# One first-layer product in another PSUM bank, and three sets of copies given to ScalarE, in a fused attention and feed-forward kernel

## The chip, the cores and the metric

The kernel runs on one NeuronCore of a Trainium2 chip. The engines named below are TensorE (PE, with its weight loads listed apart as PEld), VectorE (DVE), ScalarE (ACT), GpSimd (POOL) and SyncE (SP). Each works through its own list of instructions in order, and waits where an instruction needs a semaphore that another engine or a transfer raises. The metric is the time of one execution on the device in microseconds; the kernel before took 298.02 us, the median of 5 runs between 297.35 and 299.05.

## The reference

Attention over a sliding window (each token sees the 32 on either side of it), 8 batches of 576 tokens, 8 heads of 64, and behind it a two-layer feed-forward product with a sigmoid form of GELU, on all 4608 tokens:

```python
scores = scale * np.matmul(q, k.transpose(0, 1, 3, 2))
mask = np.abs(pos[:, None] - pos[None, :]) <= window          # window = 32
scores = np.where(mask, scores, -1000000000.0)
attn = np.exp(scores - np.max(scores, axis=-1, keepdims=True))
attn = attn / (np.sum(attn, axis=-1, keepdims=True) + 1e-09)
attn_out = np.matmul(attn, v)
...
x = attn_out.transpose(0, 2, 1, 3).reshape(4608, 512)
h = x @ w_in                                                  # 512 x 2048
g = h * (1.0 / (1.0 + np.exp(-1.702 * h)))
return g @ w_out                                              # 2048 x 512
```

## The kernel before

The tokens are taken as 36 units of 128 queries, and two units make one tile of 256 tokens for the feed-forward part. A unit passes through these steps: `scores` (PE multiplies keys with queries, ACT takes the exponential), `band` (DVE multiplies the mask in), `values` (PE multiplies with the values), `norm` (DVE divides by the sum: a reciprocal and a product for each half of the heads, which give the tile `x`), and `x_T` (x is transposed on PE, and an engine copies it from PSUM into the tile `xT`; from unit 8 on a transposing DMA does this). Then `layer1(t, d)` makes an eighth of the first layer of tile t: 8 matmuls into one PSUM bank (`h_ps`, line 332), and one ACT instruction that applies the GELU and writes `g` (line 334). `layer2`, and from tile 3 on `product`, make the second layer.

**PSUM.** The eight banks are dealt out by `bank` under four names: two called h (for first-layer products), one o, one t, and four called a, which scores and values use in turn. Under one name the banks go round: a new use waits until the use before it in the same bank has been read out. With two h banks, the third `layer1` in a row waits for the GELU of the first.

**The values.** A unit's 128 queries are two blocks of 64, and the second block needs keys that start 64 tokens later. So each 128 rows of values stand in SBUF twice: as loaded (`ve`, a ring of eight), and shifted by 64 rows (`vo`). `odd_v(m, eng)` makes the shifted copy by two copies of 64 partitions x 528 elements: the lower half of `ve[m]`, and the upper half of `ve[m + 1]`. It must come after the loads of both and before `values(m)`.

**The order** is written out by hand: the engines run their instructions in the order in which the program issues them. `head` handles units 0 to 6 and prepares the operands; then `window(4)` to `window(19)` follow. Three places matter here.

- In `head`, lines 511 to 525: first-layer products of tile 0 stand between the values of units 2 and 3 and their transposes: `layer1(0, 0)`, `values(2)`, `norm(2)`, `layer1(0, 1)`, `values(3)`, `norm(3)`, `x_T(2)`, `layer1(0, 2)`, `x_T(3)`, `layer1(0, 3)`, then tile 1. This is where ACT changes from the exponential to the GELU, and so loads another function table.
- In `head`, lines 552 to 578: `x_T(4)` and `x_T(5)` stand between the last pieces of the second layer of tiles 0 and 1, and `layer1(2, 0)` after them needs both copies. In the kernel before, unit 4's copy is DVE's and unit 5's is ACT's.
- In `window(4)`: after the scores of units 7, 8 and 9, the call `gelu_table` makes ACT load the GELU table ahead of need, by an activation of one element (`spark`). DVE masks and divides for units 7 to 9. `x_T(7)` is transposed on PE and copied by ACT, two `layer1` of tile 3 follow, DVE pairs the heads of the fourth block of queries and keys (eight copies, `qc` and `kc`), and makes the shifted values of units 10 and 11 (line 643). Then four rounds follow of `keys_T`, `queries_T` and a `layer1`. All four `keys_T` are transposed into the one t bank, so a round's transposes wait until DVE has copied the keys of the round before into `kT`.

Of the kernel before, what the change touches and what calls it, by code (L numbers as in the profile page):

```python
# [15 lines left out]
F32 = mybir.dt.float32  # L16
# [12 lines left out]
class _Kernel:  # L29
# [290 lines left out]
        self.cast(eng or nc.vector, out, tp)  # L320


    def layer1(self, t, d):
        nc = self.nc
        if d == 0:
            self.g[t] = self.work.tile([128, self.NFF, 256], F16, name="g", tag="g", bufs=2)
        hps = self.bank("h", [128, 2, 256], F32, "h_ps")
        ffs = (d, d + 8) if t > 2 else (2 * d, 2 * d + 1)
        for i in range(2):
            ff = ffs[i]  # L330
            for kr in range(self.NK):
                nc.tensor.matmul(hps[:, i, :], self.w_in_sb[:, kr, ff * 128:(ff + 1) * 128], self.xT[t][:, kr, :],  # L332
                                 start=(i == 0 and kr == 0), stop=(i == 1 and kr == self.NK - 1))
        nc.scalar.activation(self.g[t][:, ffs[0]:ffs[1] + 1:ffs[1] - ffs[0], :], hps, AF.Gelu_apprx_sigmoid)  # L334
# [105 lines left out]
    def head(self):  # L440

        nc, dve, act, pool = self.nc, self.nc.vector, self.nc.scalar, self.nc.gpsimd
# [72 lines left out]
        self.values(3)  # L515
        self.norm(3)
        self.x_T(2, "t")
        self.layer1(0, 2)
        self.x_T(3, "o")
        self.layer1(0, 3)  # L520
        for d in range(4):
# [13 lines left out]
        def run(n):  # L535
            for _ in range(n):
                l2.pop(0)()
# [20 lines left out]
        self.norm(5)  # L558
        self.band(6)
        run(1)  # L560
        self.x_T(4, "a")
        run(1)
        self.x_T(5, "a", act)
        run(1)
# [30 lines left out]
    def window(self, w):  # L595
        nc, dve, sp = self.nc, self.nc.vector, self.nc.sync
        a, b = 2 * w, 2 * w + 1
        att = w < self.NW
        t, act = w - 2, nc.scalar
        l1 = [(lambda d=d: self.layer1(w - 1, d)) for d in range(8)] if w <= self.NW else []  # L600

        def run(lst, n=1):
            for _ in range(min(n, len(lst))):
                lst.pop(0)()

        def loads():
            for m in (2 * w + 6, 2 * w + 7):
                if m < self.NU:
                    self.load_v(m)
            if w % 2 == 0 and 512 * (w // 2 + 3) < self.N:  # L610
                self.load_keys(w // 2 + 3)
                self.load_heads(w // 2 + 3, "q")

        if w == 4:
            l2 = [(lambda u=u, i=i: self.layer2(u, i, "oh"[u % 2], (dve, act)[u % 2])) for u in (4, 5) for i in range(4)]
            self.scores(7)
            self.scores(a)
            run(l2, 3)
            self.band(7)
            self.scores(b)  # L620
            run(l2)
            self.band(a)
            self.values(7, "th")
            self.gelu_table()
            self.band(b)
            self.norm(7)
            run(l2, 2)
            self.values(a)
            self.values(b)
            run(l2)  # L630
            self.x_T(7, "t", nc.scalar)
            self.norm(a)
            self.x_T(a)
            self.norm(b)
            self.x_T(b)
            run(l2)
            loads()
            run(l1, 2)
            for c in "qk":
                for hp in range(4):  # L640
                    self.pair_heads(c, 3, hp, dve)
            for m in (10, 11):
                self.odd_v(m, dve)
            run(l1, 2)
            for hp in range(4):
                self.keys_T(3, hp)
                self.queries_T(3, hp, "a", nc.scalar)
                run(l1)
            self.g_sums(w - 1, 0)
            self.feed(w)  # L650
            return
        loads()
        if not att:
            self.close(w, l1)
            return
        self.scores(a)
        if w > 5:
            self.scores(b)
        self.g_sums(t, 1, (0, 1))
        self.product(t, 1, "o")  # L660
        self.keep(t, 1, dve)
        self.product(t, 2, "h")
        if w == 5:
            self.scores(b)
        self.g_sums(t, 1, (2, 3))
        self.result(t, 11)
        self.gelu_table()
        self.product(t, 5, "t")
        self.band(a)
        self.product(t, 6)  # L670
        self.band(b, 0)
        self.keep(t, 6, dve)
        self.band(b, 1)
        run(l1)
        self.values(a)
        self.values(b)
        self.norm(a)
        self.x_T(a)
        self.product(t, 7)
        self.keep(t, 7, dve)  # L680
        self.result(t, 22)
        run(l1, 1)
        self.product(t, 4)
        self.result(t, 21, act)
        self.norm(b)
        self.x_T(b)
        self.product(t, 3)
        self.result(t, 12)
        run(l1, len(l1) - 4)
        self.g_sums(w - 1, 0)  # L690
        self.feed(w)
        run(l1, 4)
# [109 lines left out]
```

## Time and profile before

| What | Value |
|---|---|
| median of 5 runs | 298.02 us (297.35 to 299.05) |
| the profiled execution: its time, and its span from first to last instruction | 297.74 us, 295.5 us |
| PE matmul busy | 287.5 us, 97% of the span |
| DVE busy | 196.8 us, 67% |
| ACT busy | 186.9 us, 63% |
| POOL busy | 86.6 us, 29% |
| granted TensorE clock | full in the whole span |
| a first-layer product's GELU on ACT (128x512) | 595 ns, 144 of them |
| a copy to `vo` on DVE (64x528) | 303 ns on average |
| an instruction that loads an activation table | 1283 ns |

A profile page tells how long each engine was busy, and follows the chain of work that ended last back to the start. "PE busy" is a share of pipelined matmuls, whose ends are modelled: a matmul row can look busy while the next is held back. So waits of PE are better read from the starts of matmuls and weight loads than from the busy share. A row of the timeline has the start and the length in us, the engine, the line, the operation, output and input with their shapes, and the number of instructions merged into the row; in brackets stands how long the engine was idle before it and what ended that.

### The profile page before, as it was taken

The page shows a single profiled execution, that of the slowest core. Times are in us where ns is not written, and L with a number is a line of the kernel's source. Part 1 is how long each engine was busy: PE and PEld are TensorE (multiplying, and loading weights), DVE is VectorE, ACT ScalarE, POOL GpSimd, SP SyncE. Part 2 cuts the span into 40 slices and gives each one's busy share as a digit, 9 for nine tenths or more (in the row PEclk, how much of TensorE's full clock was granted, in tenths as well). Part 3 has the DMA queues.
Part 4 walks back from the last instruction along what each step waited for, and adds up shares of the span by engine and source line. Part 5 has one row for each costly group of instructions (what it writes and reads, how often), then busy time and mean ns, then how long its engine had stood idle before and what let it go on. Part 6 is the DMA issues. An engine that isn't in the chain of part 4 may idle for free.

```text
span 295.5 us, 9582 instructions
## 1 busy us (share of the span) xinstructions
PE 287.5 (97%) x4052; PEld 236.3 (80%) x4052; DVE 196.8 (67%) x589; ACT 186.9 (63%) x309; POOL 86.6 (29%) x127
## 2 busy tenths in 40 slices
PE   8889999999999999999999999999999999999994
PEld 3568755775788888888888888888888888888884
DVE  3563457788796867586768676858685858583352
ACT  4676537686684848485858585757575757575330
POOL 8876425968438011911161011202000000000000
PEclk9999999999999999999999999999999999999999
DMA  9999999999999997999499939691953030303012
GB/s 148 147 206 206 199 184 133 193 176 185 155 168 116 162 164 145 135 170 203 69 156 180 204 38 142 109 158 26 143 109 106 3 108 10 104 9 100 2 71 71
DMA packets 118649, 37.76 MB, mean 128 GB/s; under 512 B 96080, under 2 KB 114256, under 8 KB 118608
## 3 DMA queue, kind: packets, MB, share of 16 engines
q0 software_dynamic: 75888, 18.16, 76.1%
q1 hardware_dynamic: 42272, 18.62, 31.1%
q8 instruction: 31, 0.51, 0.7%
q10 hardware_dynamic: 448, 0.39, 0.5%
q14 instruction: 10, 0.08, 0.1%
HBM read 36.96 MB, written 9.44 MB: 157 GB/s over the span
## 4 chain that ended last, share of the span: by engine, by line
PE 88%; DVE 5%; ACT 2%; DMA 2%; POOL 1%; issue 1%; POOLq 0%; DVEq 0%
PE h_ps L332 41%; PE o_ps L394 31%; PE o_ps L344 6%; PE sc L263 4%; PE pv L292 3%; PE tp L176 2%; DMA ve<-in_v_dram 2%; DVE x L304 1%; ACT p L269 1%; DVE vo L106 1%; DVE qc L106 1%; DVE kT L106 1%; PE tp L319 0%; DVE p L281 0%; ACT L334 0%
## 5 line engine op out<-in xcount | busy, mean ns | idle before, releaser
L332 PE MATMUL h_ps<-xT,w_in_sb 128*128 128x256 bf16 x1152 | 135.8, 273 | 0.7 <-ACT g L334 0.7
L334 ACT ACTIVATE g<-h_ps 128x512 f16<-128x512 f32 x144 | 85.6, 595 | 74.0 <-PE h_ps L332 72.7
L332 PEld LDWEIGHTS <-w_in_sb 128*128 128x128 bf16 x1152 | 111.9, 98 | 14.3 <-issue 0.9
L157 POOL DMA_DIRECT2D ve<-in_v_dram x40 | 34.0, 861 | 100.3 <-PE pv L292 89.1
L394 PEld LDWEIGHTS <-gs 128*128 128x128 f16 x480 | 45.9, 98 | 5.7
L394 PE MATMUL o_ps<-w_sum,gs 128*128 128x256 f16 x360 | 44.4, 273 | 0.0
L269 ACT ACTIVATE p<-sc 128x512 bf16<-128x512 f32 x72 | 37.2, 604 | 2.7 <-PE sc L263 2.5
L394 PEld LDWEIGHTS <-g 128*128 128x128 f16 x360 | 34.2, 98 | 4.5 <-ACT g L334 0.2
L371 DVE TENSOR_TENSOR gs<-g 128x512 f16<-128x512 f16 x30 | 12.7, 422 | 31.6 <-ACT g L334 31.6
L304 DVE TENSOR_TENSOR x<-pv,rec 128x256 bf16<-128x256 f32 x72 | 30.6, 425 | 2.5
L394 PE MATMUL o_ps<-w_out_sb,g 128*128 128x256 f16 x240 | 29.1, 273 | 0.0
L412 DVE TENSOR_TENSOR o_sb<-o_ps,part 128x256 f32<-128x256 f32 x45 | 19.0, 422 | 12.0 <-PE o_ps L394 11.4
L106 DVE COPY part<-o_ps 128x256 f32<-128x256 f32 x45 | 19.1, 424 | 11.8 <-PE o_ps L394 10.4
L281 DVE TENSOR_TENSOR p<-p,mask 128x512 bf16<-128x512 bf16 x64 | 24.8, 427 | 1.2 <-ACT p L269 1.0
L344 PE MATMUL o_ps<-w_out_sb,g 128*128 128x512 f16 x96 | 23.2, 380 | 0.0
L106 DVE COPY vo<-ve 64x528 bf16<-64x528 bf16 x65 | 19.7, 303 | 2.8 <-DMA ve<-in_v_dram 1.3
L146 POOL DMA_DIRECT2D ks<-in_k_dram x22 | 18.6, 871 | 3.6 <-DMA qs<-in_q_dram 2.0
L431 ACT ACT_TABLE_LOAD x15 | 19.2, 1283 | 0.3
L269 ACT ACT_TABLE_LOAD x15 | 19.2, 1283 | 0.3
L303 DVE RECIPROCAL rec<-pv 128x4 f32<-128x4 f32 x72 | 12.6, 175 | 9.9 <-PE pv L292 9.9
L106 DVE COPY kT<-tp 128x512 bf16<-128x512 bf16 (+3 forms) x24 | 12.2, 530 | 7.0 <-PE tp L176 6.4
L292 PEld LDWEIGHTS <-p 128*64 128x64 bf16 x576 | 11.1, 110 | 6.4 <-DVE p L281 3.2
(69 smaller groups left out, 260.6 us busy)
## 6 DMA issues: line engine op xcount, KB each, us to landing
out_dram<-o_sb SPq DMA_DIRECT2D x34, 256.0 KB, 2.8
ve<-in_v_dram POOLq DMA_DIRECT2D x32, 128.0 KB, 5.8
ks<-in_k_dram POOLq DMA_DIRECT2D x19, 128.0 KB, 8.6
w_in_sb<-in_moe_w_in_dram POOLq DMA_DIRECT2D x4, 512.0 KB, 10.8
w_out_sb<-in_moe_w_out_dram POOLq DMA_DIRECT2D x4, 512.0 KB, 12.0
qs<-in_q_dram POOLq DMA_DIRECT2D x2, 448.0 KB, 11.5
qs<-in_q_dram POOLq DMA_DIRECT2D x3, 256.0 KB, 8.5
qs<-in_q_dram POOLq DMA_DIRECT2D x2, 384.0 KB, 11.0
```

Of the source, the lines that this page charges most:

```text
L106: (eng.copy if eng is self.nc.scalar else eng.tensor_copy)(out, in_)
L157: self.nc.gpsimd.dma_start(self.ve[m % NV][off:off + n, :, :self.D], self.v[b, :, s:s + n, :].rearrange("h s d -> s h d"))
L269: nc.scalar.activation(p[:, eo].rearrange("k h (s j) -> k h s j", j=JT), sc[eo].rearrange("k h (j s) -> k h s j", j=JT), AF.Exp, scale=sel ...
L281: self.nc.vector.tensor_mul(pv, pv, msk.to_broadcast([128, 4, 2, SQ]))
L292: nc.tensor.matmul(acc[half][blk * 64:blk * 64 + 64, hh, :], p[:, h % 2, h // 2 * 2 + blk, :], vt[:, h, :D + 1], start=(hh == 0), stop=(hh ...
L304: nc.vector.tensor_mul(x[:, hs, :], acc[half][:, :, :D], rec[:, hs, :].to_broadcast([128, 4, D]))
L332: nc.tensor.matmul(hps[:, i, :], self.w_in_sb[:, kr, ff * 128:(ff + 1) * 128], self.xT[t][:, kr, :], start=(i == 0 and kr == 0), stop=(i = ...
L334: nc.scalar.activation(self.g[t][:, ffs[0]:ffs[1] + 1:ffs[1] - ffs[0], :], hps, AF.Gelu_apprx_sigmoid)
L344: nc.tensor.matmul(o_ps, self.g[t][:, ff, s * 128:(s + 1) * 128], self.w_out_sb[:, ff, :], start=(ff == 0), stop=(ff == self.NFF - 1))
L394: nc.tensor.matmul(self.part[t, key], x, y, start=(first and k == 0), stop=(k == 7), skip_group_check=True)
L412: self.nc.vector.tensor_add(dst, self.part[t, src], self.part[t, other])
L431: self.nc.scalar.activation(self.spark, self.spark, AF.Gelu_apprx_sigmoid)
```

## The change

Three edits in the order of work; nothing is computed otherwise.

- `layer1` takes the name of the bank as an argument. `layer1(0, 2)` uses one of the four banks called a instead of an h bank.
- The copy of unit 4's transposed x goes from DVE to ACT.
- The four copies that make the shifted values of units 10 and 11 go from DVE, where they stood behind the pairing of the heads, to ACT, where they stand right after the early load of the GELU table and ahead of the copy of unit 7's transposed x.

```diff
-    def layer1(self, t, d):
+    def layer1(self, t, d, kind="h"):
         nc = self.nc
...
-        hps = self.bank("h", [128, 2, 256], F32, "h_ps")
+        hps = self.bank(kind, [128, 2, 256], F32, "h_ps")
...
         self.x_T(2, "t")
-        self.layer1(0, 2)
+        self.layer1(0, 2, "a")
         self.x_T(3, "o")
         self.layer1(0, 3)
...
-        self.x_T(4, "a")
+        self.x_T(4, "a", act)
         run(1)
         self.x_T(5, "a", act)
...
             self.gelu_table()
+            for m in (10, 11):
+                self.odd_v(m, act)
             self.band(b)
             self.norm(7)
...
                     self.pair_heads(c, 3, hp, dve)
-            for m in (10, 11):
-                self.odd_v(m, dve)
             run(l1, 2)
```

PE, POOL and SP keep their instructions in the same order. DVE has five copies fewer and ACT five more.

## The prediction

> **What bounds the kernel.** I read three views in turn: the chain of waits on the page, PE's waits, and the timeline around each wait that the change touches. The chain:
>
> ```profile
> PE 88%; DVE 5%; ACT 2%; DMA 2%; POOL 1%; issue 1%; POOLq 0%; DVEq 0%
> ```
>
> PE's issue order is the bound; 12% of the chain is something else. Where? The busy times by stretch give PE 211.00 of 211.00 us between 79 and 290 us, so nothing can be won or hidden there: whatever time PE reaches 79 us early, it ends early, if no load is late. Before 20 us the change does nothing. Between 20 and 80 us the idle times of the weight loads are:
>
> ```profile
> engine line waited for: us in total, times, longest us
> ...
> PEld L176 <- DVE kT L106: 0.9, 1, 0.9
> PEld L332 <- issue: 0.9, 1, 0.9
> ...
> PEld L332 <- DVE xT L106: 0.4, 1, 0.4
> ```
>
> These are one stall in a set of key transposes, and two in first-layer products. Each edit touches one of them.
>
> **Edit A, the bank of `layer1(0, 2)`.** The timeline at 21 us:
>
> ```profile
> 21.49 0.40 PE L319 MATMUL tp<-ident,x 128*128 128x128 bf16 x4
> ...
> 21.67 0.10 PEld L332 LDWEIGHTS <-w_in_sb 128*128 128x128 bf16 x1
> ...
> 21.98 1.09 ACT L334 ACTIVATE g<-h_ps 128x512 f16<-128x512 f32 x2
> ...
> 22.63 1.03 PE L332 MATMUL h_ps<-xT,w_in_sb 128*128 128x256 bf16 x8 [0.75 <-ACT g L334]
> ```
>
> The weights of `layer1(0, 2)` are loaded at 21.67, and its first matmul starts only at 22.63, after the first GELU (21.98 + 0.60 = 22.58), which had waited for four exponentials and a table load. Four transposes start 0.055 us apart (21.49 to 21.67), so the matmul could have started at 21.72: the wait costs 22.63 - 21.72 = 0.91 us. In the a bank nothing holds it: the bank's use before was the first half of `values(2)`, which DVE read at 20.33 to 20.75.
>
> What is late next? Eight matmuls (0.109 each, from 1.03 = 7 steps + 0.27) issue until 22.59. Then `x_T(3)` needs both halves of x(3), which DVE finishes at 22.11 and 22.66; its last two transposes wait some 0.06. `layer1(0, 3)` then starts near 22.82, against 23.73 before. It takes the h bank whose GELU ended at 22.58; `layer1(1, 0)` at 23.69 takes the one read by 23.07 and needs DVE's copy of x(3), due about 23.45. So **A gains 0.91 us**. Further on, the weights and heads that PE meets before 53 us land ahead of it: the last quarter of `w_in` at 12.4 + 12.6 = 25.0, used about 30; the paired queries of block 1, DVE's at 36.51 to 37.67, first used at 38.0 when shifted. One load becomes late, that of the values 7 (issued 34.50, 10.5 to landing: 45.0). DVE's sixth odd copy would reach it at 44.3; the mask behind it then shifts by 0.4 instead of 0.91, but ends by 47.2, and the values product that needs its first two instructions starts about then with those done since 46.2. No cost.
>
> **Edit B, x of unit 4.**
>
> ```profile
> 53.30 0.11 PEld L332 LDWEIGHTS <-w_in_sb 128*128 128x128 bf16 x2 [0.39 <-DVE xT L106]
> ```
>
> The row says 0.39, but PE was still issuing: its last second-layer matmul started at 53.02, and such steps are 0.216 us, so the product could have started at 53.24. The wait is 0.06 us. On ACT, unit 4's copy (0.59) fits into the 0.53 of idle time ahead of unit 5's (52.58 to 53.17), which then ends in time for 53.24; if ACT's two copies don't overlap at all, unit 5's ends some 0.05 later and the gain is gone. **B: -0.06**, bounds -0.06 and +0.05. The DVE time freed reaches nobody who waits.
>
> **Edit C, the odd values.** What it removes from DVE, and what it adds to ACT:
>
> ```profile
> 69.26 0.20 ACT L431 ACTIVATE spark<-spark 128x1 f32<-128x1 f32 x1
> ...
> 71.74 0.59 ACT L106 COPY xT<-tp 128x512 bf16<-128x512 bf16 x1 [2.28 <-PE tp L319]
> ...
> 72.40 3.66 PE L332 MATMUL h_ps<-xT,w_in_sb 128*128 128x256 bf16 x32
> ...
> 75.59 1.67 DVE L106 COPY vo<-ve 64x528 bf16<-64x528 bf16 x4
> ...
> 77.19 0.81 DVE L106 COPY kT<-tp 128x512 bf16<-128x512 bf16 x2
> ...
> 78.05 0.23 PEld L176 LDWEIGHTS <-kc 128*128 128x128 bf16 x4 [0.95 <-DVE kT L106]
> ```
>
> *Removed.* The second round's transposes wait for the t bank, which DVE empties at 77.19 to 78.00, behind the four copies. PE itself was free when the first round's product had been issued: it starts at 76.34, and eight steps of 0.109 end at 77.21. The stall is 78.05 - 77.21 = 0.84 us. Without the copies DVE starts on `kT` as in the next rounds, 0.43 us after the first transpose (78.05 to 78.48), so at 75.90 + 0.43 = 76.33, ends at 77.14, and PE follows at about 77.20: nothing of the stall is left. Later rounds keep pace with PE (1.3 us each).
>
> *Added.* The four copies go into ACT's idle 2.28 us (69.46 to 71.74), and what is queued behind them is the copy of unit 7's x, for which all of tile 3's first layer waits: it ends at 72.33 and PE starts at 72.40 without a pause. So the cover has no slack. Does it hold? Copies of this kind on ACT exist in the head of the trace:
>
> ```profile
> 11.04 1.28 ACT L106 COPY vo<-ve 64x528 bf16<-64x528 bf16 x2
> ```
>
> Two of 0.63 take 1.28, so they start 0.65 apart. By this row four take 3 x 0.65 + 0.63 = 2.58 and end at about 72.06, and x(7) follows. A copy from PSUM behind one from SBUF began 0.09 before the latter's end (qT at 6.50, behind a cast that ran from 5.98 to 6.60), so x(7) runs from 71.97 to 72.56 instead of 72.33: PE loses 0.2. The Trainium skill speaks for less: "ScalarE: Activation LUTs", section "What ACT_TABLE_LOAD costs", has back-to-back instructions overlap by about 93 ns. Then they are 0.535 apart, start at about 69.37, end at 71.60, and cost nothing. The trace has such overlap where ACT reads PSUM (two GELUs in 1.09 us, at 21.98), but not in the one pair that reads SBUF. I take the row: +0.2, bounds 0 and +0.4.
>
> A rule of the same page speaks against C: "Rules for kernel authors" wants simple arithmetic on VectorE, which it calls up to about 3 times faster per element in bf16. The rows agree (0.29 on DVE, 0.63 on ACT), and by engine time C would lose 4 x 0.34 = 1.36 us. But ACT's copies replace idle time up to the 0.2 counted above, and DVE's stood in front of PE. The place decides, not the price. **C: -0.84 + 0.20 = -0.64 us.**
>
> The inputs are there: the values 10, 11 and 12 are issued at 54.33, 57.86 and 58.74 and land 5.3, 9.0 and about 9.2 us later, the last at 67.9; ACT reaches the copy that needs it after 70. The copies bring no further table load: ACT's list has none added.
>
> **The sum.** -0.91 - 0.06 - 0.64 = -1.61 us. Of the profiled execution (297.74 us, which is its span of 295.5 and 2.2 around it) this leaves 296.13; the runs' median is 0.28 higher, and from it I forecast 298.02 - 1.61 = 296.4.
>
> **The rivals.** A measurement of this kernel can tell 0.3% (0.89 us) from no change, so faster means under 297.13.
>
> 1. *The sum as above*: 296.4, chance 0.46; its own range is 296.0 to 297.0.
> 2. *ACT's copies overlap*: C is -0.84, the sum -1.81, the time 296.2. For it: the PSUM pairs; against it: the SBUF pair. Chance 0.24.
> 3. *The shift is taken up by loads.* The DMA row of the page is at nine tenths for most of the first 100 us, and a PE that comes 0.9 us early may meet a load that doesn't. Against it: of all waits of PE after 20 us none is for a DMA, and the landings above have over a microsecond to spare on PE. If A and B vanish, C's 0.64 to 0.84 stay: 297.2 to 297.4, no change. That A's product finds its a bank still held would end the same way. Chance 0.22.
> 4. *Slower: ACT, standing in line, waits for the landing of the values 12.* Nothing of this stood in front of unit 7's x before. If they land at T, the fourth copy and x(7) follow, and PE starts at T + 1.27; against a start at 72.40 - 0.97 that is late by T - 70.16, and with the gains of 1.81 the net is T - 71.97. It is slower by 0.89 from T = 72.9 on, 14.1 us after the issue. The slowest load of values in the trace took 13.4 us (72.1, net +0.2). At T = 73.5 the time is 299.5. Chance 0.08.
>
> Cases 1 and 2 give faster 0.70, case 3 same 0.22, case 4 slower 0.08. The range holds cases 1 and 2 and most of case 3: 295.9 to 297.6.
>
> **What would show it.** In the profile after: `layer1(0, 2)` starting within 0.1 us of its weight load and `layer1(0, 3)` near 22.8; PE 0.9 us ahead at 53 us; four `vo` rows on ACT from about 68.4, 0.65 apart (case 1) or 0.53 (case 2), then x(7); the second round's transposes following their product without a wait; and the same lead, about 1.6 us, at 79 and at 290 us. A lead that is gone between 25 and 69 us says case 3; a gap on ACT inside the `vo` rows says case 4.

## The result, and the profile after

The changed kernel took 297.17 us in the median of 43 runs, against 298.02 in 80 runs of the kernel before. The comparison, which leaves disturbed runs out, gives a ratio of 0.9961 with a 95% interval of 0.9946 to 0.9976: 1.2 us faster (0.7 to 1.6). In two later series the ratio was 0.9921 (0.9891 to 0.9951) and 0.9969 (0.9940 to 0.9997). The forecast was 1.6 us, with 296.4 us; the median of 297.17 lies inside the stated range of 295.9 to 297.6, and just outside the 296.0 to 297.0 that case 1 gave itself.

The profiled execution took 297.17 us with a span of 295.3, only 0.2 less than before. So the two profiles must be read stage by stage. The chain of waits on the page has less of VectorE (5% before), and more of DMA (2% before):

```profile
PE 89%; DMA 5%; POOL 2%; DVE 2%; ACT 1%; issue 1%; POOLq 0%; DVEq 0%
```

Edit A, in the timeline at 21 us (start, length, engine, line, operation; this execution had come to this place 0.2 us later than the one before):

```profile
21.88 0.81 PEld L332 LDWEIGHTS <-w_in_sb 128*128 128x128 bf16 x8
...
21.93 1.04 PE L332 MATMUL h_ps<-xT,w_in_sb 128*128 128x256 bf16 x8
22.19 1.57 ACT L334 ACTIVATE g<-h_ps 128x512 f16<-128x512 f32 x3
```

The product starts 0.05 us after its weights begin to load, while the first GELU has not begun. The transposes of x(3) follow, and `layer1(0, 3)` starts at 23.05. From 21.93 the eight matmuls, 0.109 us apart, and the four transposes, 0.055 apart, fill that time.

Edit C, in the timeline of the same execution:

```profile
68.73 2.59 ACT L106 COPY vo<-ve 64x528 bf16<-64x528 bf16 x4
...
71.23 0.57 ACT L106 COPY xT<-tp 128x512 bf16<-128x512 bf16 x1
...
71.86 3.65 PE L332 MATMUL h_ps<-xT,w_in_sb 128*128 128x256 bf16 x32
...
75.79 1.04 PE L332 MATMUL h_ps<-xT,w_in_sb 128*128 128x256 bf16 x8
...
76.65 0.23 PEld L176 LDWEIGHTS <-kc 128*128 128x128 bf16 x4
```

Four copies take 2.59 us, so they do not overlap. Unit 7's x ends at 71.80, and PE starts at 71.86, some 0.2 late: its last second-layer steps began at 70.78, and four of 0.216 end at 71.64. VectorE now waits 0.66 us for PE before the first `kT`, and the second key transposes follow their product (75.79 + 8 x 0.109 = 76.66) without a pause.

What the page of before has nothing of stands at 115 us. The transposing DMA in the chain of waits (start, length), and the product behind it:

```profile
109.25 5.94 DMA xT<-x
...
115.33 0.93 PE L332 MATMUL h_ps<-xT,w_in_sb 128*128 128x256 bf16 x7 [0.86 <-DMA xT<-x]
```

PE waits for x of unit 13, issued by SyncE at 109.25 and landed at 115.19; without the wait it would have started near 114.31, one step of 0.109 after its matmul before. The same place in the kernel before:

```profile
109.68 1.23 SPq L315 DMA_TRANSPOSE xT<-x  x1
...
115.70 1.04 PE L332 MATMUL h_ps<-xT,w_in_sb 128*128 128x256 bf16 x8
```

There x had landed at 114.44, 4.76 us after its issue, and PE asked for it at 115.70.

Since every execution reaches 20 us at another time (of the profiles read here, the first first-layer product starts between 18.35 and 19.45 us), leads are best compared as lengths of stages. The products at line 332 are counted here in their order of issue, and a length runs from the first matmul of one product to that of another:

| Stage, products | what it holds | before | after | after, another execution |
|---|---|---|---|---|
| 0 to 3 | edit A | 4.95 | 4.06 | 4.07 |
| 3 to 16 | edit B | 29.58 | 29.51 | 29.51 |
| 16 to 24 | unit 7's x behind ScalarE's copies | 19.10 | 19.30 | 19.29 |
| 24 to 31 | the second key transposes | 8.75 | 7.90 | 7.90 |
| 31 to 47 | windows 4 to 6 | 29.42 | 29.41 | 29.42 |
| 47 to 48 | the wait for x of unit 13 | 5.14 | 6.16 | 5.43 |
| 48 to 143 | the rest | 168.05 | 168.08 | 168.07 |

Up to product 47 the change takes 0.89 + 0.07 - 0.20 + 0.85 = 1.61 us, which is the forecast. Then 1.02 us are given back in one execution, and 0.29 in the other.

Two things make that wait. Counted from the first first-layer product, PE was ready for x of unit 13 1.59 us earlier than before (95.33 against 96.92), but SyncE issued it only 0.63 us earlier (90.27 against 90.90). That alone leaves 0.3 us to spare. But x also took 5.94 us to land, where it had taken 4.76; with 4.76 there would have been no wait. In the other execution it took 5.29.

### The profile page after: what moved, and what is told of

Same layout as the page of the kernel before. It is cut to its first block, busy times and chain, and to the rows that moved or that the text cites. A ratio compares the mean times of both kernels' runs of the same rounds, so it can differ in the third digit from the quotient of the medians.

```text
span 295.3 us, 9589 instructions
## 1 busy us (share of the span) xinstructions
PE 287.7 (97%) x4052; PEld 236.5 (80%) x4052; DVE 195.1 (66%) x584; ACT 189.6 (64%) x314; POOL 86.9 (29%) x127
## 4 chain that ended last, share of the span: by engine, by line
PE 89%; DMA 5%; POOL 2%; DVE 2%; ACT 1%; issue 1%; POOLq 0%; DVEq 0%
PE h_ps L332 42%; PE o_ps L394 30%; PE o_ps L344 7%; PE pv L292 4%; PE sc L263 4%; DMA qs<-in_q_dram 3%; DMA xT<-x 2%; PE tp L176 2%; POOL ve L157 1%; PE tp L319 0%; POOL ks L138 0%; DVE qc L106 0%; DVE o_sb L412 0%; POOL neg L237 0%; ACT qT L106 0%
## 5 line engine op out<-in xcount | busy, mean ns | idle before, releaser
L106 DVE COPY vo<-ve 64x528 bf16<-64x528 bf16 x61 | 18.2, 299 | 3.2 <-DMA ve<-in_v_dram 1.8
```

The source lines that it names most:

```text
L106: (eng.copy if eng is self.nc.scalar else eng.tensor_copy)(out, in_)
```

## The experiments

The theory going in: the four sizes above are the edits' own and add up; what is missing from 1.61 us is the wait for x of unit 13. It stands in SyncE's queue behind the transposes of block 4, so it comes earlier by less than PE does. The rivals: the lead is taken up by loads in any case; or the difference lies elsewhere.

**A alone** (`a_bank`): the kernel before with `self.layer1(0, 2, "a")`.

> Before, with the bank of layer1(0, 2) alone changed. My theory: PE starts that product within 0.1 us of its weight load and is 0.91 us ahead of the kernel before at layer1(0, 3) and still at 79 us; the transposed x of unit 13 lands at about 114.4 us, some 1.2 us before PE asks for it, so a lead of 0.9 meets no wait there and reaches the end: 0.9 us less (ratio 0.997). Rival (loads that don't come earlier take up any lead): PE waits for a transposing DMA near 115 us also here, and 0.3 us or less is left.

Stage 0 to 3 took 4.07 us (0.88 less than before), and stage 47 to 48 the same 5.14: no wait at 115 us. Here x of unit 13 took 4.40 us and landed 2.08 us before PE's use. The ratio was 0.9993 (0.9968 to 1.0017). That holds the expected 0.997 and no change alike, so the time alone doesn't settle it.

**B alone** (`b_x4`): the kernel before with `self.x_T(4, "a", act)`.

> Before, with the copy of unit 4's x alone given to ScalarE. My theory: layer1(2, 0) starts 0.06 us earlier against the second-layer matmul ahead of it, nothing else moves; the time can't tell it from no change. Rival (the 0.39 us that the wait list gives for the weight load is real): layer1(2, 0) starts 0.3 to 0.4 us earlier.

Stage 3 to 16 took 29.51 us, 0.07 less: the theory's size, not the 0.39 of the wait list. One run took 297.17 us. But the same stage took 29.71 in `a_bank`, 29.84 in `hold` below, and 29.51 in `c_odd`, all without B. With B it was 29.51 in every profile read here. In these four profiles without B, the listed idle time of that weight load goes with the stage (0.7 us in `hold`, 0.5 in `a_bank`, 0.4 before, 0.3 in `c_odd`). So what B removes is a wait of 0 to 0.3 us that comes and goes, and the 0.06 was one draw of it.

This run showed two more things. Stage 24 to 31 took 8.08 us with nothing changed there, where before had 8.75. VectorE's odd copies took 1.25 us for four, not 1.67.

And stage 0 to 3 took 5.60 us. The busy times by stretch show why (stretch in us, its length, busy time of PE, PEld, DVE, ACT and POOL, granted clock, DMA share, GB/s):

```profile
18.00:20.00 2.00, 1.87 (x47) 1.39 (x47) 0.00 (x0) 1.66 (x4) 1.88 (x5) 0.68 1.24 206
20.00:22.00 2.00, 2.00 (x24) 1.28 (x23) 1.00 (x4) 1.97 (x3) 1.78 (x9) 0.50 1.24 209
```

The granted clock was 0.68 and 0.50 in the 4 us in which A acts; in the profile before it was 1.00. PE is slower there, and comes to the product that A moves 4.43 us after the first product (2.89 before). By then the wait is over, though this kernel has no A. The first GELU ended at 22.32 (21.72 + 0.60), and the product started 0.05 us after its weights began to load:

```profile
23.09 0.81 PEld L332 LDWEIGHTS <-w_in_sb 128*128 128x128 bf16 x8
...
23.14 1.04 PE L332 MATMUL h_ps<-xT,w_in_sb 128*128 128x256 bf16 x8
```

So A has nothing to remove in an execution with such a dip. The four profiles that have both A and a dip (`f_defer`, `k_defer`, `ks`, `hold_abk`) say the same: the first GELU ended 0.4 to 0.6 us before that product's weights were loaded. Their stage 0 to 3 took 5.21 to 5.45 us. That this is below 5.60 is no gain of A: all of the difference lies ahead of the product, which is 1.11 to 1.12 us before product 3 in all five. In the four the dip, 3.4 us long, began before the stage, and in `b_x4` all of it lies inside.

**C alone** (`c_odd`): the kernel before with the odd values of units 10 and 11 on ScalarE.

> Before, with the odd values of units 10 and 11 alone given to ScalarE. My theory: four copies 0.65 us apart on ScalarE, PE starts layer1(3, 0) 0.2 us late behind unit 7's copy, the 0.84 us wait of the second key transposes is gone, net lead 0.6 us at 79 us; no DMA wait near 115 us, so 0.6 us less at the end (ratio 0.998). Rival (loads take up any lead): a DMA wait near 115 us, and nothing is left.

Stage 16 to 24 took 19.29 us (0.19 more) and stage 24 to 31 7.90 (0.85 less), with no wait at 115 us (x of unit 13 took 4.57 us, and landed 1.49 us before its use). The ratio, 0.9995 (0.9974 to 1.0015), again can't tell 0.6 us from nothing.

**Three transposes deferred** (`f_defer`): the changed kernel with

```diff
-                self.queries_X(i)
-            for c in ((2, 3) if w % 2 else (0, 1)):
+                if w > 5:
+                    self.queries_X(i)
+            if w == 6:
+                self.queries_X(4)
+                for c in (2, 3):
+                    self.keys_X(4, c)
+            for c in ((2, 3) if w % 2 else (0, 1)) if w != 5 else ():
                 self.keys_X(i, c)
```

> The changed kernel, with the three transposing DMAs that the end of window 5 puts on SyncE (queries of block 4, two quarters of keys of block 4) issued at the end of window 6 instead, so behind the transposes of x of units 12 and 13. My theory: what the changed kernel's profile lost of its lead (1.6 us at 79 us, 0.5 at 115) was the wait for x of unit 13, which SyncE issued at 109.3 us behind these three, though it was ready at 104.4. Here it is issued before 107 us, the wait at 115 us is gone, the lead of 1.6 us stays, the span is 293.6 to 294.0 us and the time 0.4 us under the changed kernel's (ratio to before 0.9945). Rival 1 (the wait is of the DMA engines, not of SyncE's order): x of unit 13 still lands after 114 us and the time is the changed kernel's, ratio 0.996. Rival 2 (the difference between forecast and measurement lies elsewhere): the wait goes and the ratio stays 0.996.

Slower than before: 301.83 us, ratio 1.0131 (1.0101 to 1.0162). Half of the theory held: x of unit 13 was issued at 106.7 and landed at 110.0, so SyncE's order bears on its landing. But the queries of block 4 landed at 115.0, and unit 15's scores need them, since its last queries lie in block 4. In the list of PE's waits (who, for whom, us in total, times, longest):

```profile
PE sc L263 <- DMA qT<-qc: 2.7, 1, 2.7
```

Stage 47 to 48 took 9.31 us; part of that is a second dip of the granted clock to 0.5, for 3.4 us from 114.5 on. No expectation had foreseen this.

**Two transposes deferred** (`k_defer`): as above, but the queries stay at the end of window 5 and only `keys_X(4, 2)` and `keys_X(4, 3)` move.

> The changed kernel with the two transposes of keys of block 4 that stand at the end of window 5 issued at the end of window 6, behind x of units 12 and 13; the queries of block 4 stay (unit 15's scores need them at 111 us). My theory: SyncE issues x of unit 13 about 4 us earlier (near 105), it lands before 112, PE never waits for it, and the keys still land before their use at 126 us. Full lead kept: 1.6 us under before (ratio 0.9945), 0.4 under the changed kernel. Rival 1: no change against the changed kernel (0.996), the landing is set by the transfer engines. Rival 2: the deferred keys are late in turn, as the queries were in the larger deferral, and it is slower than before.

SyncE's timeline in this kernel:

```profile
107.34 1.23 SPq L315 DMA_TRANSPOSE xT<-x  x1
...
109.28 6.01 SPq L151 DMA_TRANSPOSE kT<-ks  x4
```

The two x (unit 12's was issued at 104.77) now stand ahead of the keys. Unit 13's landed at 112.0, and stage 47 to 48 was 5.14 us, though stages 3 to 47 were as short as in the changed kernel. Its stage 0 to 3 had the dip, so PE came to product 47 only 0.2 us ahead of before, and a wait was less likely here anyway. The landing says more: 4.2 us before its use, where the kernel before had 1.26. The ratio was 0.9940 (0.9912 to 0.9969), as expected; the changed kernel beside it (`again`, 7 runs) had 0.9921 (0.9891 to 0.9951), so the times don't show the deferral to be faster.

**The changed kernel again** (`again`, beside `k_defer`; `again2`, in the last series).

> The changed kernel, once more. My theory: what varies between executions is when the transposed x of unit 13 lands (112.3 to 115.2 us in the five profiles so far), and PE waits for it only where it lands after 114.3; so the lead at 79 us is again 1.4 to 1.6 us against the start of layer1(0, 1), and is kept in this profile if x lands earlier. Rival (the wait belongs to the change): x lands near 115.2 again and PE waits some 0.9 us near 115 us.

Of `again` only the times above are read, not the stages.

> The changed kernel beside the two combinations on the same chip. As forecast: 1.2 to 1.6 us under the kernel before; four odd copies 0.65 us apart on ScalarE, layer1(3, 0) 0.2 us late, and a wait near 115 us only if x of unit 13 lands after PE's need.

The stages of `again2` are the last column of the table. PE was ready for the product of unit 13 near 114.07 and started at 114.36; x had landed at 114.23. The profile's list of waits doesn't put this one down to a DMA; but the start is 0.14 us after the landing, as it is in the changed kernel's first profile, where the list does.

**Only unit 10 on ScalarE** (`s_split`): `self.odd_v(10, act)` after the table load, `self.odd_v(11, dve)` after the four rounds of key transposes.

> The changed kernel with only unit 10's odd values on ScalarE; unit 11's go back to VectorE, behind the four rounds of key transposes. My theory: two copies end 1.3 us earlier, so unit 7's x is not delayed and PE starts layer1(3, 0) 0.2 us earlier than in the changed kernel; VectorE's two copies near 80.5 us meet no one. 0.2 us less than the changed kernel at 79 us, which the time can hardly tell. Rival (the copies behind the rounds hold up the sums of g, and these PE): PE later by 0.3 us or more after 82 us.

Stage 16 to 24 went back to 19.09 us: the 0.2 us is the price of the third and fourth copy. But stage 31 to 47 took 29.87 instead of 29.41. VectorE's two copies run into its densest stretch, 80 to 87 us, and the mask of unit 11 comes later: PE waits for it before the values product. Here the rival was right, with 0.46 us. Stage 47 to 48 was 6.49 us, as x of unit 13 took 6.73 us to land. The ratio was 0.9969 (0.9948 to 0.9990).

**GpSimd held back** (`hold`): the kernel before, with GpSimd's loads of keys and queries of window 4 placed behind VectorE's odd copies. In front of these loads GpSimd copies eight elements of the last odd values, so that it waits for them (the code here is cut; the earlier `loads()` is reduced to its two loads of values):

```diff
+            held = self.cst.tile([128, 8], BF16, name="held")
+            nc.gpsimd.tensor_copy(held, self.vo[11 % NV][:, 0, 0:8])
+            self.load_keys(5)
+            self.load_heads(5, "q")
```

> The kernel before, with GpSimd's loads of keys and queries of window 4 held back until VectorE has made the odd values of unit 11 (GpSimd reads eight elements of them first). Theory: part of the 0.84 us that PE waited for the second key transposes is time in which VectorE's copies between SBUF tiles stood still while GpSimd issued loads (single copies of 0.56 to 0.72 us beside 0.28 to 0.30); with the loads held, eight head copies take 2.3 us instead of 2.7, the four odd copies 1.3 instead of 1.7, and PE's wait is 0.2 us or less: 0.65 us gained by this alone. The loads come 5 us later, which may make x of unit 13 land later. Rival (the slow copies have another cause): the copies keep their lengths and the wait is 0.8 us.

VectorE's copies and GpSimd's loads in the kernel before (the odd copies, 1.67 us, follow at 75.59):

```profile
71.74 3.13 POOL L146 DMA_DIRECT2D ks<-in_k_dram  x4
...
72.94 1.56 DVE L106 COPY qc<-qs 128x512 bf16<-128x512 bf16 x4
74.42 1.17 DVE L106 COPY kc<-ks 128x512 bf16<-128x512 bf16 x4
```

And in `hold`:

```profile
73.01 0.89 DVE L106 COPY qc<-qs 128x512 bf16<-128x512 bf16 x4
73.81 0.89 DVE L106 COPY kc<-ks 128x512 bf16<-128x512 bf16 x4
74.72 1.23 DVE L106 COPY vo<-ve 64x528 bf16<-64x528 bf16 x4
...
76.01 0.19 POOL L646 COPY held<-vo 128x8 bf16<-128x8 bf16 x1 [4.34 <-DVE vo L106]
```

Twelve copies, each 0.28 to 0.30 us, and `kT` waits 0.45 us for PE, not for the copies. Stage 24 to 31 took 7.91 us: the whole wait is gone with all four odd copies still on VectorE. In the kernel before, the same twelve took 0.27 to 0.72 each. The Trainium skill ("SBUF — State Buffer", section "Who interferes with whom") says that VectorE's copies in their two-port modes and GpSimd exclude each other from one pair of ports, each for a whole instruction. This case agrees in the times: the copies lengthen by up to some 0.4 us where GpSimd issues loads, and don't where it waits. Neither the mode of these copies nor the ports can be seen in a trace here.

Yet the ratio of `hold` to before was 1.0007 (0.9982 to 1.0032), against the 0.8 us that stage 24 to 31 shows. In this execution 0.26 us of the stage lead went in stage 3 to 16; the other 0.6 lies just outside the interval, which allows 0.5, and what takes it back in the other runs is not shown.

**Two combinations.** `ks` is `s_split` with the deferral of `k_defer`. `hold_abk` is the kernel before with A, B, `hold` and that deferral, without C.

> The changed kernel with both earlier improvements: unit 11's odd values back on VectorE behind the four rounds, and the two transposes of keys of block 4 deferred behind x of units 12 and 13. My theory: no wait of PE for unit 7's x (0.2 us less at 73 us than the changed kernel), no wait for x of unit 13 near 115 us, lead 1.8 us at 79 us against the start of layer1(0, 1), and kept to the end: 0.3 to 0.6 us under the changed kernel run beside it. Rival: the same time as the changed kernel, whose executions mostly don't meet the wait.

> The kernel before with the bank of layer1(0, 2) and unit 4's copy changed, the odd values of units 10 and 11 left on VectorE, GpSimd's loads of window 4 held behind them, and the two key transposes deferred. My theory: the second key transposes wait less than 0.1 us though VectorE still makes all four odd copies, since these run at 0.29 us each; unit 7's x is not delayed; lead 1.8 us at 79 us, kept to the end unless the later loads bring x of unit 13 after 114 us. Same time as the other combination. Rival (the odd copies have to leave VectorE for the gain): the wait of the second key transposes is 0.5 us or more.

| Kernel | stage 16 to 24 | 24 to 31 | 31 to 47 | 47 to 48 | ratio to before (interval) |
|---|---|---|---|---|---|
| `again2` | 19.29 | 7.90 | 29.42 | 5.43 | 0.9969 (0.9940 to 0.9997) |
| `ks` | 19.09 | 7.91 | 29.70 | 5.14 | 0.9954 (0.9924 to 0.9984) |
| `hold_abk` | 19.09 | 7.90 | 29.41 | 5.14 | 0.9960 (0.9935 to 0.9985) |

`hold_abk` has the shortest of every stage in the table: 0.2 us less than the changed kernel before x of unit 13, and no wait for it. `ks` pays 0.3 for unit 11's copies behind the rounds. With the keys deferred, x of unit 13 landed 4.0 us (`ks`) and 5.0 (`hold_abk`) before its use. But both profiles have the dip in stage 0 to 3 (5.41 and 5.21 us, against 4.07 in `again2`), so neither shows the full lead. The times don't tell the three apart.

## Why the prediction was right, and where it was off

- **A, 0.91 us**: 0.89 and 0.88 in executions at full clock. What I had not seen is that the granted clock can dip at 18 to 22 us, and that the wait A removes is then not there: PE comes to the product after the GELU has ended (`b_x4`).
- **B, 0.06 us**: 0.07 against the profile before. Its true size is between 0 and 0.3, by the execution. Reading it from matmul starts instead of the listed 0.39 was right.
- **C, what it adds, 0.20 us**: 0.20, from four copies 0.65 us apart. The row of two copies in the head decided rightly against the overlap that the Trainium skill gives in "ScalarE: Activation LUTs", section "What ACT_TABLE_LOAD costs" (case 2).
- **C, what it removes, 0.84 us**: 0.85 against that profile. But the profile before was near the upper end: the same wait measured 0.73 (`a_bank`) and 0.18 (`b_x4`) in other executions. The prediction took one execution's wait as the wait. It even had the cause in view, since the four copies took 1.67 us where 4 x 0.29 is 1.2.
- **The sum, 1.61 us, kept to the end**: this is the step that failed, as the lead was not kept. The sum up to product 47 was 1.61, and 1.02 and 0.29 of it went into the wait for x of unit 13. I had written that PE's full busy share after 79 us means nothing can be lost "if no load is late", and then looked only at loads before 79 us. The view of before gave the warning: x of unit 13 landed 1.26 us ahead of PE's need, less than the lead of 1.61. It did not settle the matter, as SyncE's issue came 0.63 us earlier too; the rest was the slower transfer. In the three profiles read that have A, B, ScalarE's copies and SyncE's order unchanged, x took 5.29 to 6.73 us and PE waited; in the five with A, B, C, `hold` or nothing alone it took 4.34 to 4.76, and PE did not. So case 3, the shift taken up by loads, came true in part and behind 79 us, not before. It named the right resource and the wrong place.
- Case 4 did not happen: ScalarE's copies ran without a gap.

That moving the transposes of the keys behind x takes this wait away is shown by `k_defer`, `ks` and `hold_abk`, where x lands 4.0 to 5.0 us before its use. Why it takes longer to land in the three profiles with the wait is not shown.

How much of the difference between 1.6 us and the measured 1.2 is the dip can be estimated, as the record gives the mean granted clock of every run. The profiles with a dip at 20 us have a mean of 0.986 to 0.994, those read without one 0.997 to 1.000. Of the runs that the comparison uses, 23 of the changed kernel are at 0.997 or above, with a median of 296.0 us, and 17 below, with 297.5. Of the kernel before, in three later series, 86 have 297.6 and 46 have 298.3. So the change gains some 1.5 us at full clock (1.1 to 1.8, by resampling the runs), and some 0.9 with a dip (0.2 to 1.2), where B and C alone would give 0.7. At full clock the forecast fits; the dips, in about four of ten runs, would account for most of what is missing. In the series with 0.9921 every run of the changed kernel that was compared was at 0.997 or above. This is a sorting of runs and not an experiment: it compares different series, and a low mean doesn't say where the dip lay. How often the wait for x of unit 13 comes, and the smaller waits that B and C meet, stays open, as there is one profile per kernel; and the times of A and C alone are too uncertain to tell.

That the result still fell into the stated range was in part luck: the range had been drawn wide enough for case 3, but the dip was in no case, and the wait was expected somewhere else.

## What to carry to other kernels

A lead that PE wins is worth only as much as the tightest transfer further on has to spare. So before adding gains, look up, for every transfer that PE will ask for afterwards, its landing in the trace against its use. Where the difference is smaller than the lead, the rest of the lead is in doubt: in an in-order queue what stands ahead of that transfer may not come as much earlier as PE does. And the difference is a draw too: it was 1.26 us before, and 1.5 to 2.6 in four other profiles with SyncE's order unchanged.

A wait of some tenths of a microsecond in one profile is one draw: compare the rows that make it up with the shortest row of the same kind. Where they differ, ask what stretches them. Taking that away may win the same without moving the work.

## What the runs showed of the hardware

- ScalarE's copies from SBUF to SBUF (64 x 528) start 0.65 us apart, one after another's end (0.63 each), in each of the profiles with C; GELUs and exponentials that read PSUM start 0.49 us apart at 0.60 each.
- VectorE's copies between SBUF tiles take 0.28 to 0.30 us where GpSimd is held back (`hold`, `hold_abk`), and up to 0.76 while it issues loads (the changed kernel).
- A transposing DMA of x keeps SyncE's queue for 1.2 us at the least; the larger one of the queries kept it for 6.0 to 6.5 us when issued at 96 to 98 us, and for 2.5 when issued at 108.6 (`f_defer`). The transfers behind it are issued after that.
- The granted clock fell to 0.5 around 20 us, for 3.4 us, in five of the profiles, and was 1.0 there in the others.
